# The last quarter of a fused read and expert layer: stored without a sum, in two halves

## The chip, the cores and the metric

The kernel runs on one core of a Trainium2 chip. The core has five engines with instruction streams of their own: TensorE (PE in the profile; its weight loads are shown as PEld), VectorE (DVE), ScalarE (ACT), GpSimd (POOL) and SyncE (SP), which here only issues transfers. The engines run at the same time and wait for one another through semaphores; each executes its own stream in order. Matmuls write to PSUM, which VectorE and ScalarE read; transfers go between SBUF and memory. The metric is the device time of one execution in microseconds, as the median of several.

## The reference

Two computations follow each other. First a cross read between tokens x and states, per batch and head, in both directions; then a two-layer expert layer with a parametric ReLU over all 4352 rows that come out (8 batches of 512 tokens and 32 states).

```python
scores = scale * np.matmul(x, state.transpose(0, 1, 3, 2))     # B, H = 8, 8; S, Ns, D = 512, 32, 64
a = np.exp(scores - scores.max(-1, keepdims=True))
a /= a.sum(-1, keepdims=True) + 1e-09
xread = np.matmul(a, state)
# the same with the roles of x and state exchanged gives sread
x = concatenate([xread, sread], axis=2) as rows of H * D = 512
h = x @ w_in                                                   # 512 x 2048
g = np.maximum(h, 0.0) + alpha * np.minimum(h, 0.0)
out = g @ w_out                                                # 2048 x 512
```

## The kernel before

The order of all work is written out by hand: a long string, ORDER, holds some 1100 tokens such as P.8.3.0.0, and a small interpreter at the end of the kernel calls one function for each, with the parts behind the name as arguments (line by line in the string, so this order is the order of each engine's stream). The interpreter turns a part that consists of digits into an integer and leaves any other part a string:

```python
for token in (globals().get("TOKENS") or ORDER).split():
    name, *args = token.split(".")
    steps[name](*[int(a) if a.isdigit() else a for a in args])
```

Blocks 0 to 7 are the tokens of the eight batches, 512 rows each. Block 8 is the states' rows of all batches, 256 rows, and comes last. For each block the first layer makes h in PSUM (F), ScalarE makes the negative part (N, line 630) and VectorE combines both to g (G, line 633).

The second layer, g times w_out, is done for block 0 directly (S and O) and for blocks 1 to 8 as a product of 2x2 blocks with seven products instead of eight (the quarters of the result are two row halves th by two column halves dh). The steps of a block b are:

- U.b.i.c, lines 696 to 715, on GpSimd: sums and differences of parts of g, named gsum_b_i_c. Each (i, c) has one buffer for all blocks, so U.8.4.0 overwrites what block 7's products of gsum_7_4_0 read.
- P.b.p.i.c, lines 717 to 743, on PE: product p for row tile i and half c of the inner dimension, four matmuls of 128x256. The products 1, 3, 5 and 6 go to the PSUM bank px_b, product 2 to py_b, products 4 and 7 to pv_b.
- K.b.n, line 752, on ScalarE: copies the state that px_b has reached at that point to SBUF, as kept_n_b; the following products go on adding to px_b.
- Q.b.th.dh, lines 760 to 770: forms a quarter of the result in SBUF (oq_b_th_dh) and stores it. The quarter (0, 0) is py plus kept_1, (1, 1) is pv plus kept_4, (1, 0) is pv plus kept_2, each as a sum on VectorE (line 769). The quarter (0, 1) is px itself and only copied, by the engine that the token names (line 767: v for VectorE, a for ScalarE). All stores are issued by SP, 256 KB for a block of tokens and 128 KB for block 8.

The sum Q.b.1.1 reads pv_b between two of its products: product 7 is in it, product 4 isn't yet. The products P.b.4 that follow write onto the bank that it reads. The buffers for oq are four, used in turn.

Of the kernel before, what the change touches and what calls it, by code (L numbers as in the profile page):

```python
# [30 lines left out]
F.1.7.1 N.0.13 tn.0.1.p W.3.1.p W.3.0.p tn.0.0.a N.1.7 G.0.12 G.0.13 G.1.7 F.1.3.3 N.1.3 W.2.1.p S.0.0.7 mo.1.3.a
S.0.1.6 O.0.1.v W.4.1.p F.1.5.0 N.1.5 S.0.3.6 G.1.3 G.1.5 F.1.2.1 N.1.2 G.1.2 F.1.15.4 N.1.15 F.1.12.3 G.1.15 N.1.12
G.1.12 m.1.2 F.1.6.0 N.1.6 G.1.6 F.1.14.1 N.1.14 G.1.14 mo.1.2.a S.0.0.4 S.0.0.6 O.0.0.a F.1.0.4 N.1.0 F.1.13.3 sc.2
sb.2 m.2.2.0.1 rd.1.2 mo.2.2.a.0 mo.2.2.a.1 rdo.1.a tm.2 S.0.3.7 tt.0 smax.2 S.0.3.5 O.0.3.a N.1.13 S.0.2.1.2 nb.2.a
S.0.2.5 te.2.1 S.0.2.6 S.0.2.7 te.2.0 F.1.1.0 N.1.1 G.1.13 F.1.8.1 N.1.8 G.1.0 G.1.1 F.1.4.5 S.0.2.2 m.3.2 G.1.8
N.1.4 G.1.4 F.1.10.0 lx.3 ssh.p.2 lst.1 sexp.2 mo.3.2.a ssum.2.1 tsum.2 S.0.2.4 S.0.2.0 F.1.9.5 rd.0.3 P.1.2.0.1.4
snorm.v.2 rdo.0.a N.1.9 G.1.9 S.0.2.3 N.1.10 P.1.1.0.1.3 P.1.1.1.1 P.1.2.1.1 xd.3 O.0.2.a tn.2.0.a m.2.3.1.2
mo.2.3.a.0 m.2.1 mo.2.3.a.1 wb.2 G.1.10 F.1.11.5 N.1.11 mo.2.1.a G.1.11 P.1.1.1.0 U.1.1.1.p str.1.1 sro.1.v tn.2.1.p
tt.2 F.2.15.2 F.2.1.0 P.1.2.0.0 P.1.1.0.0 F.2.14.5 m.3.1 N.2.15 N.2.1 G.2.15 K.1.1.a N.2.14 mo.3.1.a G.2.1 G.2.14
m.3.0.1.2 mo.3.0.v.1 P.1.2.1.0 F.2.11.0 U.1.3.1.p mo.3.0.a.0 U.1.2.1.p P.1.6.1.1 N.2.11 F.2.2.5 N.2.2 F.2.0.2 N.2.0  # L40
U.1.1.0.p U.1.2.0.p U.1.4.0.p lx.4 P.1.6.0.1 Q.1.0.0 G.2.11 m.5.0.1.4 mo.5.0.a.0 G.2.2 mo.5.0.a.1 rd.2.0 rdo.2.a
G.2.0 sc.3 m.3.3.5.1 mo.3.3.a.1 tm.3 mo.3.3.v.0 m.4.0.4.2 mo.4.0.a.1 sb.3 P.1.6.1.0 P.1.6.0.0 xd.4 F.2.13.0 F.2.7.1
mo.4.0.a.0 F.2.8.2 K.1.2.a P.1.5.1.0 N.2.7 nb.3.a G.2.7 N.2.13 G.2.13 N.2.8 G.2.8 F.2.9.5 N.2.9 G.2.9 te.3.0
P.1.5.0.0 smax.3 P.1.7.1.1.4 F.2.10.1 N.2.10 F.2.5.0 N.2.5 G.2.5 G.2.10 F.2.4.2 N.2.4 G.2.4 te.3.1 P.1.5.1.1
U.1.3.0.p P.1.7.1.0 P.1.5.0.1 K.1.4.a U.1.4.1.p F.2.3.5 N.2.3 G.2.3 P.1.7.0.1 F.2.6.0 N.2.6 ssh.p.3 lx.5 F.2.12.1
# [57 lines left out]
def kernel(  # L103
# [658 lines left out]
    def quarter_out(b, th, dh, e=None):  # L762
# [3 lines left out]
        if add is None:  # L766
            copier(e)(osb, pbanks[b, name])
        else:
            nc.vector.tensor_tensor(osb, pbanks[b, name], kept[b, add], ALU.add)  # L769
# [51 lines left out]
```

## Time and profile before

| what | value |
|---|---|
| median of three runs | 209.41 us (209.22 to 210.38) |
| span of the profiled execution (first to last instruction) | 207.1 us |
| median less this span | 2.3 us |
| mean granted TensorE clock | 0.996 |
| PE busy | 200.4 us, 97% |
| GpSimd, VectorE, ScalarE busy | 179.5, 171.7, 155.3 us |
| last matmul ends | 203.39 us |
| last sum on VectorE ends | 203.85 us |

The page gives no time of the profiled execution besides its span. Its parts are the busy time of each engine, the span in 40 slices, the chain of work that ended last, groups of instructions by line, and transfers. A row of the timeline gives start, duration, engine, line, operation, result and operands (buffer numbers left out) and how many instructions it holds; in brackets stands how long the engine idled ahead of it, and what ended that. The tile names there are short: px is px_7 as well as px_8, oq is any quarter.

### The profile page before, as it was taken

To read this page: it belongs to the slowest core of one execution; us is meant where nothing else is said; L and a number is where in the kernel's file an instruction comes from. 1 tells how busy PE (TensorE), PEld (TensorE's weight loads), DVE (VectorE), ACT (ScalarE), POOL (GpSimd) and SP (SyncE) were. 2 spreads that over 40 slices of the span, in tenths; PEclk is the share of its full clock that TensorE was granted. 3 is DMA by queue.
4 is the path that set the end of the run, shared out by engine and by line. 5 is a ranking of instruction groups with operands and counts; after the bars stand their busy time and mean duration, and the time that the engine had idled before them with its cause. 6 is when DMAs were issued, how large, how long until landed. Compare 5 with 4: busy or idle time off the path is not lost.

```text
span 207.1 us, 5034 instructions
## 1 busy us (share of the span) xinstructions
PE 200.4 (97%) x1997; PEld 133.6 (65%) x1997; DVE 171.7 (83%) x251; ACT 155.3 (75%) x306; POOL 179.5 (87%) x113
## 2 busy tenths in 40 slices
PE   7899999999999999999999999999999999999992
...
GB/s 175 215 207 205 204 204 97 158 173 106 178 82 101 116 192 156 53 38 167 243 118 104 148 105 0 54 103 152 55 0 53 102 0 3 0 101 104 101 77 125
DMA packets 44038, 23.68 MB, mean 114 GB/s; under 512 B 22256, under 2 KB 43504, under 8 KB 44016
## 3 DMA queue, kind: packets, MB, share of 16 engines
...
## 4 chain that ended last, share of the span: by engine, by line
PE 86%; DVE 5%; ACT 4%; DMA 2%; issue 1%; ACTq 0%
PE px L736 26%; PE h L577 24%; PE pv L736 13%; PE py L736 7%; PE m_ps L528 4%; PE h L586 3%; PE o L647 3%; DVE g L633 3%; DMA x<-in_x_dram 2%; PE sr_ps L501 2%; PE fill L253 2%; ACT neg L630 1%; PE sc L335 1%; ACT m L554 1%; PE xT_ps L320 1%
## 5 line engine op out<-in xcount | busy, mean ns | idle before, releaser
L633 DVE SCALAR_TENSOR_TENSOR g<-neg,oma_sb,h 128x512 f16<-128x512 f32 (+1 forms) x142 | 94.0, 711 | 11.6 <-ACT neg L630 11.0
L630 ACT ACTIVATE neg<-h 128x512 f32<-128x512 f32 (+1 forms) x142 | 75.6, 580 | 16.5 <-PE h L577 11.5
L577 PE MATMUL h<-aT,m 128*128 128x512 f16 x252 | 66.8, 380 | 0.1
L736 PEld LDWEIGHTS <-gsum 128*128 128x128 f16 x480 | 46.5, 98 | 13.1 <-issue 0.9
L736 PEld LDWEIGHTS <-g 128*128 128x128 f16 x360 | 34.7, 98 | 8.8 <-issue 1.4
L715 POOL TENSOR_TENSOR gsum<-g,g 128x1024 f16<-128x1024 f16 (+1 forms) x16 | 32.1, 2007 | 6.7 <-DVE g L633 4.9
L577 PEld LDWEIGHTS <-m 128*128 128x128 f16 x252 | 23.8, 98 | 18.4 <-issue 2.0
L715 POOL TENSOR_TENSOR gsum<-g,gsum 128x1024 f16<-128x1024 f16 (+1 forms) x16 | 32.0, 2005 | 1.5 <-PE px L736 1.0
L715 POOL TENSOR_TENSOR gsum<-gsum,g 128x1024 f16<-128x1024 f16 (+1 forms) x16 | 32.1, 2007 | 1.0
L736 PE MATMUL px<-ws,gsum 128*128 128x256 f16 x240 | 32.1, 273 | 0.0
L715 POOL TENSOR_TENSOR gsum<-g 128x1024 f16<-128x1024 f16 (+1 forms) x16 | 31.9, 2006 | 0.0
L752 ACT COPY kept<-px 128x512 f32<-128x512 f32 (+1 forms) x24 | 13.6, 567 | 21.0 <-PE px L736 20.9
L554 ACT CAST m<-m_ps 128x512 f16<-128x512 f32 x35 | 19.1, 602 | 1.5 <-PE m_ps L528 1.1
L769 DVE TENSOR_TENSOR oq<-pv,kept 128x512 f32<-128x512 f32 (+1 forms) x16 | 10.4, 649 | 10.6 <-PE pv L736 10.4
L736 PE MATMUL px<-w_out_sb,gsum 128*128 128x256 f16 x120 | 17.2, 273 | 0.0
L736 PE MATMUL px<-w_out_sb,g 128*128 128x256 f16 x120 | 17.2, 273 | 0.0
L405 POOL TENSOR_TENSOR ts<-ts,mx 128x1024 f32<-128x1024 f32 x7 | 13.3, 1911 | 4.4 <-DVE mx L400 4.4
L647 PE MATMUL o<-w_out_sb,g 128*128 128x512 f16 x64 | 16.6, 380 | 0.1
L736 PE MATMUL py<-w_out_sb,g 128*128 128x256 f16 x120 | 16.6, 273 | 0.0
L736 PE MATMUL pv<-ws,gsum 128*128 128x256 f16 x120 | 16.4, 273 | 0.0
L736 PE MATMUL pv<-ws,g 128*128 128x256 f16 x120 | 15.9, 273 | 0.0
L552 ACT CAST m<-m_ps 128x1024 f16<-128x1024 f32 x13 | 13.2, 1018 | 0.5 <-PE m_ps L528 0.4
...
## 6 DMA issues: line engine op xcount, KB each, us to landing
...
out_dram<-oq SPq DMA_DIRECT2D x4, 128.0 KB, 2.1
...
```

The lines of the kernel that those rows point to most:

```text
L405: engine(e).tensor_tensor(blocks(cols(live["ts", b], j, S)), blocks(scored(b, j)), over_blocks(cols(live["mx", b], j, S // N)), ALU.subtract,)
L528: nc.tensor.matmul(t[N * k : N * (k + 1), :], st_head(b, h)[64 * r : 64 * r + 64, :], w_in_sb[64 * r : 64 * r + 64, c, 512 * f : 512 * (f ...
L552: copier(e)(m_tile(b, f), t)
L554: copier(e)(m_tile(b, f)[:, g, :], t[g])
L577: nc.tensor.matmul(h.rearrange("p (r j s) -> p r j s", r=2, j=2), ms[b, f][:, g, 128 * j : 128 * (j + 1)], weights(b, g), start=(g == 0), ...
L630: nc.scalar.activation(neg, h, RELU, bias=0.0, scale=-1.0)
L633: nc.vector.scalar_tensor_tensor(g_tile(b, jc), negs.pop((b, jc)), oma_sb[:, jc : jc + 1], hs.pop((b, jc)), ALU.mult, ALU.add,)
L647: nc.tensor.matmul(outs[b, q], g_tile(b, jc)[:, 128 * q : 128 * (q + 1)], w_out_sb[:, jc, :], start=not begun and jc == 2 * jc2, stop=left ...
L715: engine(e).tensor_tensor(t, x(), y(), op)
L736: nc.tensor.matmul(pbanks[b, name][:, i, :], of(b, c)[:, j, 128 * i : 128 * (i + 1)], moving[:, 4 * c + j, :], start=not begun and j == 0, ...
L752: copier(e)(t, pbanks[b, "x"])
L769: nc.vector.tensor_tensor(osb, pbanks[b, name], kept[b, add], ALU.add)
```

## The change

Three things are written into the kernel.

First, the end of ORDER. The token P.7.3.0.0 moves behind P.8.3.0.1, and Q.7.0.1 (the copy of px_7) stays right behind it. The last product of the quarter (0, 1) of block 8, P.8.3.0.0, moves behind P.8.4.0.0, and so does its quarter's token, which is now the last of all. Second, that quarter is made in a new manner, "h": VectorE copies its left 128 columns and ScalarE its right 128, each half into its part of the same buffer, and each half is stored by a transfer of its own, the left by SP, the right by ScalarE's queue. Third, the tokens of three quarters of block 1 get a fourth part, 2, and a store of two row tiles is to be issued as two when this part is there.

```diff
-lx.4 P.1.6.0.1 Q.1.0.0 G.2.11 ...
+lx.4 P.1.6.0.1 Q.1.0.0.2 G.2.11 ...
...
-... m.6.0 Q.1.1.1 m.4.1.2.5 ...
+... m.6.0 Q.1.1.1.2 m.4.1.2.5 ...
...
-... U.2.2.1.p Q.1.1.0 U.2.4.1.p ...
+... U.2.2.1.p Q.1.1.0.2 U.2.4.1.p ...
...
-P.8.6.0.1 P.8.6.0.0 P.7.3.1.0 P.8.2.0.0 P.7.3.0.0 K.8.2.a P.8.5.0.1 U.8.3.1.p Q.8.0.0 P.8.5.0.0 K.8.4.a
-P.8.7.0.0.4 P.8.7.0.1 Q.7.0.1.v P.8.3.0.1 U.8.4.0.p Q.8.1.1 P.8.3.0.0 P.8.4.0.1 Q.8.0.1.a P.8.4.0.0 Q.8.1.0
+P.8.6.0.1 P.8.6.0.0 P.7.3.1.0 P.8.2.0.0 K.8.2.a P.8.5.0.1 U.8.3.1.p Q.8.0.0 P.8.5.0.0 K.8.4.a
+P.8.7.0.0.4 P.8.7.0.1 P.8.3.0.1 P.7.3.0.0 Q.7.0.1.v U.8.4.0.p Q.8.1.1 P.8.4.0.1 P.8.4.0.0 Q.8.1.0 P.8.3.0.0 Q.8.0.1.h
...
         osb = moe.tile([128, n_i, d_h], F32, name=f"oq_{b}_{th}_{dh}", tag="osb", bufs=4)
+        if e == "h":
+            to = quarter_rows(b, th, dh)
+            for i, (copy, queue) in enumerate(((nc.vector.tensor_copy, nc.sync), (nc.scalar.copy, nc.scalar))):
+                part = slice(d_h // 2 * i, d_h // 2 * (i + 1))
+                copy(osb[:, 0, part], pbanks[b, name][:, 0, part])
+                queue.dma_start(to[:, :, part], osb[:, 0, part])
+            return
         if add is None:
             copier(e)(osb, pbanks[b, name])
         else:
             nc.vector.tensor_tensor(osb, pbanks[b, name], kept[b, add], ALU.add)
-        nc.sync.dma_start(quarter_rows(b, th, dh), osb if b < B else osb[:, 0, :])
+        to = quarter_rows(b, th, dh)
+        if b < B and e == "2":
+            for i in range(n_i):
+                nc.sync.dma_start(to[:, i, :], osb[:, i, :])
+        else:
+            nc.sync.dma_start(to, osb if b < B else osb[:, 0, :])
```

What this makes of the streams is read from the built programs, in their order and without times. A row names the line, the operation, the result and operands and the shape, and in brackets the semaphores that it waits for. PE's last products before, one matmul of each four:

```order
L736 MATMUL py_8_3347<-w_out_sb_91,g_8_2_2977 128x256
...
L736 MATMUL px_7_3170<-w_out_sb_91,gsum_7_4_0_3305 128x256
...
L736 MATMUL px_8_3366<-ws_1_430,gsum_8_1_1_3362 128x256 [waits Activation_49]
...
L736 MATMUL px_8_3366<-ws_1_430,gsum_8_1_0_3371 128x256
...
L736 MATMUL pv_8_3442<-ws_3_604,gsum_8_3_0_3326 128x256
...
L736 MATMUL pv_8_3442<-ws_3_604,gsum_8_3_1_3431 128x256
...
L736 MATMUL px_8_3366<-w_out_sb_91,gsum_8_4_1_3392 128x256 [waits Activation_49]
...
L736 MATMUL px_8_3366<-w_out_sb_91,gsum_8_4_0_3458 128x256
...
L736 MATMUL pv_8_3442<-ws_4_570,g_8_3_2756 128x256 [waits DVE_49]
...
L736 MATMUL pv_8_3442<-ws_4_570,g_8_2_2977 128x256
```

And now (the lines stand one lower, since ORDER is one line shorter):

```order
L735 MATMUL py_8_3347<-w_out_sb_91,g_8_2_2977 128x256
...
L735 MATMUL px_8_3366<-ws_1_430,gsum_8_1_1_3362 128x256 [waits Activation_49]
...
L735 MATMUL px_8_3366<-ws_1_430,gsum_8_1_0_3371 128x256
...
L735 MATMUL pv_8_3438<-ws_3_604,gsum_8_3_0_3326 128x256
...
L735 MATMUL pv_8_3438<-ws_3_604,gsum_8_3_1_3427 128x256
...
L735 MATMUL px_8_3366<-w_out_sb_91,gsum_8_4_1_3392 128x256 [waits Activation_49]
...
L735 MATMUL px_7_3170<-w_out_sb_91,gsum_7_4_0_3305 128x256
...
L735 MATMUL pv_8_3438<-ws_4_570,g_8_3_2756 128x256 [waits DVE_49]
...
L735 MATMUL pv_8_3438<-ws_4_570,g_8_2_2977 128x256
...
L735 MATMUL px_8_3366<-w_out_sb_91,gsum_8_4_0_3458 128x256
```

The product on px_7 has moved right ahead of the pv product that waits for VectorE, and the product of gsum_8_4_0 has moved to the end.

VectorE's last rows before:

```order
L769 TENSOR_TENSOR oq_7_1_0_3402<-pv_7_3281,kept_2_7_3307 128x512 [waits DMAHW2_49,DVE_49,PE_49]
L769 TENSOR_TENSOR oq_8_0_0_3433<-py_8_3347,kept_1_8_3390 128x256 [waits DMAHW3_49,PE_49,Activation_49]
L767 COPY oq_7_0_1_3451<-px_7_3170 128x512 [waits DMAHW4_49,DVE_49,PE_49]
L769 TENSOR_TENSOR oq_8_1_1_3460<-pv_8_3442,kept_4_8_3440 128x256 [waits DVE_49,DMAHW5_49,PE_49,Activation_49]
L769 TENSOR_TENSOR oq_8_1_0_3478<-pv_8_3442,kept_2_8_3425 128x256 [waits DMAHW7_49,DVE_49,PE_49]
```

And now:

```order
L775 TENSOR_TENSOR oq_8_0_0_3429<-py_8_3347,kept_1_8_3390 128x256 [waits DMAHW3_49,PE_49,Activation_49]
L773 COPY oq_7_0_1_3455<-px_7_3170 128x512 [waits DMAHW4_49,DVE_49,PE_49]
L775 TENSOR_TENSOR oq_8_1_1_3460<-pv_8_3438,kept_4_8_3436 128x256 [waits DMAHW5_49,DVE_49,Activation_49]
L775 TENSOR_TENSOR oq_8_1_0_3471<-pv_8_3438,kept_2_8_3421 128x256 [waits DMAHW6_49,DVE_49,PE_49]
L769 COPY oq_8_0_1_3478<-px_8_3366 128x128 [waits DMAHW7_49,DVE_49,PE_49]
```

The copy of px_7 keeps its place ahead of the sum oq_8_1_1, and the copy of a half is new at the end.

ScalarE's last rows now (before, the last was one copy oq_8_0_1 of 128x256, which waited for two transfers and PE):

```order
L751 COPY kept_4_7_3352<-px_7_3170 128x512 [waits PE_49,Activation_49]
L751 COPY kept_1_8_3390<-px_8_3366 128x256 [waits DVE_49,PE_49,Activation_49]
L751 COPY kept_2_8_3421<-px_8_3366 128x256 [waits DVE_49,PE_49,Activation_49]
L751 COPY kept_4_8_3436<-px_8_3366 128x256 [waits PE_49,Activation_49]
L769 COPY oq_8_0_1_3478<-px_8_3366 128x128 [waits DMAHW5_49,DMAHW6_49,DMAHW3_49,DMAHW7_49,DMAHW1_49,DVE_49]
L770 DMA out_0_dram<-oq_8_0_1_3478 32x4x128 [waits DMAHW4_49,Activation_49]
```

The copy of the right half waits for VectorE's semaphore, and a transfer has come to ScalarE's queue. SP's last rows now:

```order
L781 DMA out_0_dram<-oq_8_0_0_3429 32x4x256 [waits DMAHW7_49,DVE_49]
L781 DMA out_0_dram<-oq_7_0_1_3455 256x1x256 [waits DMAHW0_49,DVE_49]
L781 DMA out_0_dram<-oq_8_1_1_3460 32x4x256 [waits DMAHW1_49,DVE_49]
L781 DMA out_0_dram<-oq_8_1_0_3471 32x4x256 [waits DMAHW2_49,DVE_49]
L770 DMA out_0_dram<-oq_8_0_1_3478 32x4x128 [waits DMAHW3_49,DVE_49]
```

Ahead of these, SP has the same transfers in the same shapes as before, those of block 1 among them, at one row each. The store of the half stands last on SP, behind oq_8_1_0.

More of the change, by code (lines that the diff above doesn't have):

```diff
@@ L31 @@
[L31 to L45, printed above, removed]
@@ new lines @@
+G.0.11 sc.0.1 sc.0.0 F.0.15.3 G.0.9 F.0.14.1 S.0.3.4 S.0.1.4 S.0.1.5 tm.0 tn.1.1.a tn.1.0.a tt.1 N.0.15 G.0.15 W.2.0.p
+N.0.14 G.0.14 wb.1 nb.0.a W.4.0.p F.0.13.0 te.0.1 te.0.0 tsum.0 F.0.12.3 N.0.12 S.0.0.5 S.0.1.7 m.1.3 F.1.7.1 N.0.13
+tn.0.1.p W.3.1.p W.3.0.p tn.0.0.a N.1.7 G.0.12 G.0.13 G.1.7 F.1.3.3 N.1.3 W.2.1.p S.0.0.7 mo.1.3.a S.0.1.6 O.0.1.v
+W.4.1.p F.1.5.0 N.1.5 S.0.3.6 G.1.3 G.1.5 F.1.2.1 N.1.2 G.1.2 F.1.15.4 N.1.15 F.1.12.3 G.1.15 N.1.12 G.1.12 m.1.2
+F.1.6.0 N.1.6 G.1.6 F.1.14.1 N.1.14 G.1.14 mo.1.2.a S.0.0.4 S.0.0.6 O.0.0.a F.1.0.4 N.1.0 F.1.13.3 sc.2 sb.2 m.2.2.0.1
@@ new lines @@
+P.1.1.0.0 F.2.14.5 m.3.1 N.2.15 N.2.1 G.2.15 K.1.1.a N.2.14 mo.3.1.a G.2.1 G.2.14 m.3.0.1.2 mo.3.0.v.1 P.1.2.1.0
+F.2.11.0 U.1.3.1.p mo.3.0.a.0 U.1.2.1.p P.1.6.1.1 N.2.11 F.2.2.5 N.2.2 F.2.0.2 N.2.0 U.1.1.0.p U.1.2.0.p U.1.4.0.p
+lx.4 P.1.6.0.1 Q.1.0.0.2 G.2.11 m.5.0.1.4 mo.5.0.a.0 G.2.2 mo.5.0.a.1 rd.2.0 rdo.2.a G.2.0 sc.3 m.3.3.5.1 mo.3.3.a.1
+tm.3 mo.3.3.v.0 m.4.0.4.2 mo.4.0.a.1 sb.3 P.1.6.1.0 P.1.6.0.0 xd.4 F.2.13.0 F.2.7.1 mo.4.0.a.0 F.2.8.2 K.1.2.a
+P.1.5.1.0 N.2.7 nb.3.a G.2.7 N.2.13 G.2.13 N.2.8 G.2.8 F.2.9.5 N.2.9 G.2.9 te.3.0 P.1.5.0.0 smax.3 P.1.7.1.1.4
@@ new lines @@
+F.2.10.1 N.2.10 F.2.5.0 N.2.5 G.2.5 G.2.10 F.2.4.2 N.2.4 G.2.4 te.3.1 P.1.5.1.1 U.1.3.0.p P.1.7.1.0 P.1.5.0.1 K.1.4.a
+U.1.4.1.p F.2.3.5 N.2.3 G.2.3 P.1.7.0.1 F.2.6.0 N.2.6 ssh.p.3 lx.5 F.2.12.1 N.2.12 G.2.6 P.1.7.0.0 P.1.3.1.0 m.6.0
+Q.1.1.1.2 m.4.1.2.5 sexp.3 P.1.3.1.1 mo.6.0.a G.2.12 mo.4.1.a.0 ssum.3.0 U.2.1.0.p snorm.v.3 P.1.3.0.0 P.1.4.0.0
+mo.4.1.a.1 P.1.3.0.1 U.2.2.0.p Q.1.0.1.a P.1.4.1.1 tsum.3 m.6.1.1.2 wb.3 mo.6.1.a.0 m.4.3 mo.4.3.a m.5.3.5.3 P.1.4.0.1
+mo.5.3.a.1 P.2.1.0.1.1 P.2.1.1.0 P.1.4.1.0 mo.5.3.a.0 sc.4 U.2.1.1.p U.2.2.1.p Q.1.1.0.2 U.2.4.1.p tn.3.0.p U.2.3.0.p
@@ new lines @@
+U.2.3.1.p tm.4 mo.6.1.a.1 m.4.2.0.3 mo.4.2.a.0 F.3.15.5 xd.5 N.3.15 G.3.15 F.3.1.2 F.3.8.4 N.3.1 G.3.1 N.3.8
+mo.4.2.a.1 P.2.1.0.0 F.3.12.0 N.3.12 G.3.8 nb.4.a P.2.1.1.1 F.3.7.5 G.3.12 F.3.6.3 K.2.1.a F.3.14.2 N.3.6 P.2.6.0.1
+P.2.6.1.1 sb.4 N.3.14 G.3.14 F.3.4.4 P.2.6.0.0 P.2.6.1.0 F.3.2.0 G.3.6 tn.3.1.a N.3.4 G.3.4 N.3.7 G.3.7 K.2.2.a te.4.1
+F.3.3.2 smax.4 F.3.0.3 te.4.0 N.3.3 G.3.3 N.3.2 G.3.2 P.2.5.0.0 P.2.5.0.1 P.2.5.1.0 N.3.0 P.2.5.1.1 K.2.4.a F.3.11.4
+F.3.9.5 sc.5 ssh.p.4 G.3.0 N.3.9 G.3.9 N.3.11 tt.3 G.3.11 rd.3.2 P.2.7.1.0.0 rdo.3.a F.3.10.3 N.3.10 P.2.2.1.0.5
@@ new lines @@
+P.2.2.0.0 tsum.4 P.2.2.0.1 U.2.4.0.p lx.6 P.2.7.1.1 tm.5 P.2.7.0.1 F.3.5.2 F.3.13.4 sexp.4 G.3.10 nb.5.a te.5.0
+U.3.1.0.p U.3.2.0.p N.3.5 tn.4.0.a ssum.4.3 P.2.7.0.0 P.2.3.1.1 Q.2.1.1 P.2.2.1.1 snorm.v.4 P.2.3.0.1 te.5.1 G.3.5
+P.2.3.0.0 P.2.4.0.0 P.2.4.1.1 tsum.5 tn.4.1.a P.2.3.1.0 N.3.13 tn.5.1.a tn.5.0.a tt.5 wb.4 G.3.13 P.2.4.0.1
+P.3.1.0.0.3 P.2.4.1.0 Q.2.1.0 Q.2.0.1.a P.3.1.0.1 F.4.3.2 Q.2.0.0 F.4.7.4 N.4.3 F.4.11.1 U.3.1.1.p F.4.5.0 N.4.7
+P.3.1.1.1 G.4.3 F.4.10.5 G.4.7 N.4.11 G.4.11 F.4.9.2 F.4.12.4 P.3.1.1.0 F.4.8.1 N.4.5 G.4.5 N.4.10 G.4.10 U.3.2.1.p
@@ new lines @@
+N.4.9 G.4.9 F.4.2.0 K.3.1.a U.3.4.1.p N.4.12 G.4.12 P.3.6.0.0 N.4.8 F.4.13.5 G.4.8 N.4.2 G.4.2 P.3.6.1.0 N.4.13
+P.3.6.0.1 m.7.0.2.4 mo.7.0.a.0 mo.7.0.a.1 sb.5 rd.5.1 rdo.5.a tt.4 rd.4.0 rdo.4.a xd.6 G.4.13 F.4.14.2 N.4.14
+P.3.6.1.1 F.4.15.4 K.3.2.a sc.6 G.4.14 m.6.3.1.0 tm.6 m.7.3.5.2 N.4.15 P.3.5.1.1 G.4.15 mo.7.3.a.0 mo.7.3.a.1
+U.3.3.0.p mo.6.3.a.1 P.3.5.1.0 F.4.6.5 N.4.6 F.4.4.2 N.4.4 sb.6 G.4.4 P.3.5.0.1 smax.5 lx.7 P.3.5.0.0 P.3.7.0.0.4
+K.3.4.a nb.6.a te.6.0 F.4.0.0 N.4.0 U.3.3.1.p F.4.1.2 N.4.1 mo.6.3.a.0 P.3.3.0.1 te.6.1 P.3.7.1.0 U.3.4.0.p P.3.7.1.1
@@ new lines @@
+G.5.7 U.4.2.1.p P.4.6.0.1 F.5.12.1 N.5.12 G.5.12 F.5.5.4 U.4.3.0.p F.5.9.2 N.5.5 G.5.5 N.5.9 G.5.9 P.4.6.1.1 F.5.10.5
+P.4.6.0.0 tm.7 P.4.6.1.0 F.5.8.1 N.5.10 F.5.1.4 F.5.14.2 K.4.2.a N.5.14 Q.4.0.0 G.5.14 P.4.5.1.1 U.4.3.1.p P.4.5.1.0
+P.4.5.0.0 G.5.10 nb.7.a wb.6 te.7.0 P.4.5.0.1 N.5.1 te.7.1 tsum.7 F.5.4.3 G.5.1 N.5.8 G.5.8 P.4.7.0.0.2 F.5.11.5
+N.5.11 G.5.11 K.4.4.a tn.7.0.a P.4.7.0.1 P.4.7.1.1 P.4.7.1.0 F.5.6.4 N.5.6 U.4.4.1.p P.4.3.0.1 P.4.3.1.1 tn.6.1.p
+F.6.2.1 N.6.2 U.4.4.0.p P.4.3.0.0 P.5.1.1.0.5 P.4.3.1.0 sb.7 Q.4.1.1 P.4.4.1.1 P.4.4.0.1 G.6.2 G.5.6 smax.7 P.4.4.0.0
@@ new lines @@
+P.4.4.1.0 tn.6.0.a Q.4.0.1.a Q.4.1.0 N.5.4 G.5.4 F.6.4.1 N.6.4 G.6.4 P.5.1.0.0 F.6.9.0 F.6.1.4 N.6.9 G.6.9 F.5.13.2
+N.5.13 tt.6 tn.7.1.p G.5.13 F.6.5.3 N.6.5 G.6.5 U.5.1.0.p P.5.1.1.1 F.6.14.1 P.5.1.0.1 U.5.2.0.p ssh.p.7 F.6.3.0
+F.6.12.2 N.6.14 G.6.14 P.5.2.0.1.3 P.5.2.1.1 tt.7 F.6.6.1 K.5.1.a P.5.6.0.0 P.5.6.1.0 P.5.2.1.0 N.6.3 G.6.3 N.6.1
+N.6.12 G.6.1 N.6.6 G.6.6 G.6.12 U.5.1.1.p U.5.2.1.p sexp.7 P.5.2.0.0 m.7.1.0.4 mo.7.1.a.1 mo.7.1.a.0 Q.5.0.0 rd.7.1
+rdo.7.a rd.6.2 rdo.6.a ssum.7.3 snorm.v.7 P.5.6.0.1 P.5.6.1.1 K.5.2.a F.8.2.4 F.8.12.0 N.8.2 G.8.2 F.6.8.1 N.6.8 G.6.8
@@ new lines @@
+F.6.15.2 N.8.12 G.8.12 U.5.4.1.p F.6.7.3 N.6.7 G.6.7 F.8.6.4 P.5.5.0.1 wb.7 F.6.13.1 N.6.13 U.5.3.1.p P.5.7.0.1.0
+P.5.7.1.1 N.8.6 G.8.6 G.6.13 P.5.5.1.0 U.5.3.0.p P.5.5.1.1 F.8.1.3 N.8.1 P.5.7.0.0 P.5.7.1.0 F.8.3.4 N.6.15 G.6.15
+N.8.3 U.5.4.0.p P.5.5.0.0 F.6.0.1 K.5.4.a G.8.3 F.8.0.2 U.6.1.1.p G.8.1 P.5.3.0.0 Q.5.1.1 N.6.0 F.7.3.4 U.6.2.1.p
+N.8.0 G.8.0 F.8.4.3 P.5.3.0.1 F.6.10.2 G.6.0 P.5.3.1.1 N.6.10 G.6.10 N.7.3 N.8.4 G.8.4 P.5.4.0.0 U.6.4.1.p F.6.11.1
+N.6.11 P.5.3.1.0 Q.5.0.1.a F.7.14.2 P.5.4.0.1 G.6.11 G.7.3 P.5.4.1.0 P.5.4.1.1 Q.5.1.0 U.6.1.0.p N.7.14 G.7.14
@@ new lines @@
+F.7.13.3 N.7.13 F.7.8.5 G.7.13 F.7.7.1 N.7.7 G.7.7 F.8.11.4 N.7.8 F.7.12.0 G.7.8 N.8.11 F.7.4.2 N.7.4 G.7.4 U.6.2.0.p
+G.8.11 P.6.1.1.0.3 U.6.3.1.p U.6.4.0.p F.8.15.1 P.6.1.0.1 F.8.8.5 N.8.8 N.8.15 P.6.1.0.0 P.6.1.1.1 K.6.1.a F.8.14.2
+F.7.5.4 N.7.12 N.7.5 P.6.6.0.0 G.7.12 G.8.8 P.6.6.1.0 G.7.5 P.6.6.0.1 F.7.6.0 N.7.6 P.6.7.1.1.5 P.6.7.0.1 G.8.15
+U.6.3.0.p G.7.6 U.7.3.1.p P.6.6.1.1 K.6.2.a F.7.0.4 N.7.0 F.8.10.1 G.7.0 N.8.10 G.8.10 P.6.5.1.0 N.8.14 G.8.14
+F.7.15.0 N.7.15 G.7.15 P.6.5.0.1 F.7.2.4 F.7.11.1 F.8.13.2 N.7.2 G.7.2 P.6.5.1.1 U.7.1.1.p N.8.13 G.8.13 N.7.11 G.7.11
@@ new lines @@
+P.6.7.1.0 F.7.1.0 N.7.1 F.8.5.4 N.8.5 G.7.1 F.7.10.2 U.7.2.1.p N.7.10 G.7.10 P.6.5.0.0 K.6.4.a P.6.2.0.0.1 G.8.5
+F.7.9.0 P.6.2.1.1 P.7.1.0.1.2 P.7.1.0.0 N.7.9 P.6.2.0.1 G.7.9 P.6.2.1.0 P.6.7.0.0 F.8.9.4 P.6.3.0.1 P.7.2.0.0.0
+P.6.3.0.0 U.7.1.0.p Q.6.1.1 P.7.1.1.1 P.6.4.0.0 P.6.4.0.1 P.6.4.1.0 Q.6.0.0 P.6.4.1.1 Q.6.1.0 P.7.1.1.0 U.7.3.0.p
+P.6.3.1.0 F.8.7.1 P.6.3.1.1 P.7.2.1.0 U.7.2.0.p K.7.1.a P.7.6.1.1 P.7.6.0.0 N.8.7 G.8.7 P.7.7.0.0.5 P.7.6.0.1
+P.7.6.1.0 P.7.7.1.0 P.7.2.0.1 Q.6.0.1.v U.7.4.0.p K.7.2.a P.7.5.1.1 P.7.5.0.1 U.7.4.1.p N.8.9 G.8.9 P.7.5.1.0
```

73 lines of the change are left out of this document (16 added, 57 removed).

## The prediction

> **What bounds the kernel now.** I read the page's head and slices first, then the chain of waits over the last 7 us, because the diff touches little else.
>
> ```profile
> span 207.1 us, 5034 instructions
> PE 200.4 (97%) x1997; PEld 133.6 (65%) x1997; DVE 171.7 (83%) x251; ACT 155.3 (75%) x306; POOL 179.5 (87%) x113
> ...
> PE   7899999999999999999999999999999999999992
> ```
>
> ```profile
> 199.90 0.87 PE px L736 x8
> 200.77 0.87 PE pv L736 x8
> 201.64 0.87 PE px L736 x8
> 202.52 0.89 PE pv L736 x8
> 203.40 0.02 issue
> 203.43 0.42 DVE oq L769
> ```
>
> TensorE (PE) is busy 97% of the span, and in every slice but the first and last. The end is a chain: PE's last products, one VectorE sum of 0.42 us, then a store. So whatever delays PE near the end is paid in full, and whatever shortens the work behind its last product is gained in full. The timeline there, in start, duration, engine:
>
> ```profile
> 199.29 0.60 PE L736 MATMUL px<-w_out_sb,gsum 128*128 128x256 f16 x4
> 199.73 1.04 PE L736 MATMUL px<-ws,gsum 128*128 128x256 f16 x8
> 200.60 1.04 PE L736 MATMUL pv<-ws,gsum 128*128 128x256 f16 x8
> 201.48 1.04 PE L736 MATMUL px<-w_out_sb,gsum 128*128 128x256 f16 x8
> 202.35 1.04 PE L736 MATMUL pv<-ws,g 128*128 128x256 f16 x8
> ...
> 199.55 0.42 DVE L769 TENSOR_TENSOR oq<-py,kept 128x256 f32<-128x256 f32 x1 [1.11 <-PE py L736]
> 199.93 0.69 DVE L767 COPY oq<-px 128x512 f32<-128x512 f32 x1
> 201.74 0.42 DVE L769 TENSOR_TENSOR oq<-pv,kept 128x256 f32<-128x256 f32 x1 [1.11 <-PE pv L736]
> 203.43 0.42 DVE L769 TENSOR_TENSOR oq<-pv,kept 128x256 f32<-128x256 f32 x1 [1.26 <-PE pv L736]
> ...
> 200.04 1.15 POOL L715 TENSOR_TENSOR gsum<-g,gsum 128x512 f16<-128x512 f16 x1 [1.04 <-PE px L736]
> ```
>
> A product of four matmuls takes PE 0.437 us (eight stand 0.87 apart), and the last of its matmuls ends 0.60 us after the first begins. PE's last end is 202.35 + 1.04 = 203.39. In this order the row at 199.29 is P.7.3.0.0, the last product of px_7. Three things hang on it or follow it: VectorE's copy of px_7 (Q.7.0.1) at 199.93; GpSimd's gsum_8_4_0 (U.8.4.0), which overwrites the one buffer that this product reads and starts 0.15 us after it; and on VectorE, in program order behind the copy, the sum Q.8.1.1 at 201.74. PE's pv products P.8.4.0.1 and P.8.4.0.0 (the row at 202.35) write onto the bank that this sum reads, so they must come after it. They do, by 202.35 - 202.16 = 0.19 us, and PE waits for nothing.
>
> **The change, part by part.**
>
> *The early stores.* The three tokens end in "2". The interpreter turns digits into integers, and the new code asks e == "2", a string. So the branch is never taken; SyncE's (SP's) rows up to the last few are the same in both programs. Cost 0, with nothing to hide.
>
> *P.7.3.0.0 goes five products later*, behind P.8.5.0.1, P.8.5.0.0, P.8.7.0.0, P.8.7.0.1 and P.8.3.0.1. Those five start 0.437 earlier each, with the same lead over what releases them; no new wait there. It itself starts at 199.29 + 5 x 0.437 = 201.48 and ends at 202.08. VectorE takes up a finished product 0.04 after its end (203.39 to 203.43), so the copy of px_7 runs from 202.12 to 202.81. The sum Q.8.1.1 is queued behind it and could before start at 201.74; now it runs from 202.81 to 203.23. PE's P.8.4.0.1 is next in PE's order, due at 201.48 + 0.437 = 201.92, and must wait for that sum. The handover from VectorE to PE, seen early in the kernel:
>
> ```profile
> 5.38 0.96 DVE L189 CAST xg<-x 128x512 f16<-128x512 f32 x2 [5.38 <-DMA x<-in_x_dram]
> ...
> 6.39 0.23 PEld L320 LDWEIGHTS <-xg 128*128 128x128 f16 x4 [0.30 <-DVE xg L189]
> ```
>
> The casts end at 6.34 and the weights behind them load at 6.39: 0.05 us. So P.8.4.0.1 starts at 203.28, a stall of 1.36 us where there was none. Could it be less? Back-to-back VectorE rows above start 0.38 apart for a 0.42 us instruction, which would give 1.32; a slower handover of 0.1 would give 1.41. I take 1.36.
>
> U.8.4.0 is moved with it: it waits for P.7.3.0.0, runs from 202.08 + 0.15 = 202.23 to 203.38, and P.8.3.0.0, now PE's last product, needs its result. That product would come at 203.28 + 2 x 0.437 = 204.15, so the sum of GpSimd is hidden by the stall. Were the stall gone, it would be what is late next: P.8.3.0.0 due at 202.79 would start at 203.38 + 0.05 = 203.43, 0.64 us late. PE's last end becomes 204.15 + 0.60 = 204.75, that is +1.36.
>
> The 256 KB store of px_7 is issued 2.19 us later, with two 128 KB stores behind it on SP. SP issues one in some 0.55 us (row below): 202.83, 203.38, and the third when its sum ends (204.35 + 0.42 = 204.77). SP is free again at 205.32. No engine waits for these.
>
> *The last quarter.* Removed from the path: the sum of 0.42 us, which now runs at 204.35 beside PE's last product. Added: a VectorE copy of 128x128, a ScalarE copy of 128x128, and a store by each engine's queue, 64 KB each. ScalarE's copy stands in the built program behind a wait for VectorE's semaphore, and the only VectorE instruction left to wait for is the other half's copy. So I take the halves one after the other.
>
> ```profile
> L767 DVE COPY oq<-px 128x512 f32<-128x512 f32 x2 | 1.4, 688 | 0.0
> L474 DVE RECIPROCAL r<-r 128x2 f32<-128x2 f32 x8 | 1.2, 145 | 0.0
> L769 DVE TENSOR_TENSOR oq<-py,kept 128x256 f32<-128x256 f32 x1 | 0.4, 425 | 1.1 <-PE py L736 1.1
> ...
> L454 ACT ACTIVATE nb<-nb 128x2 f32<-128x2 f32 x8 | 1.7, 208 | 0.0
> L767 ACT COPY oq<-px 128x256 f32<-128x256 f32 x1 | 0.4, 372 | 1.3 <-PE px L736 1.3
> L275 ACT CAST st<-st 128x128 f16<-128x128 f32 x1 | 0.3, 292 | 0.0
> ```
>
> No 128x128 copy runs on VectorE: between 0.145 (two columns) and 0.425 (256). The line through 256 and 512 columns gives 0.29, which I take. ScalarE: between 0.208 and 0.372; the cast of the same size took 0.292, taken as 0.28. So 204.75 + 0.04 + 0.29 = 205.08 for the first half, + 0.05 + 0.28 = 205.41 for the second; before, the last data stood ready at 203.43 + 0.42 = 203.85. That is +1.56; by the bounds of the two copies +1.34 to +1.79, and +1.23 if the halves ran side by side. The Trainium skill, PSUM — Partial Sum Buffer, section "PSUM bank collisions raise a hardware error", says that two engines must not access one bank in the same 32 partitions at once, two reads included, and that a semaphore has to keep them apart. By that rule the split saves nothing over one copy; the sum with halves side by side would be 0.33 us less. The trace of before has no pair of such reads.
>
> ```profile
> L770 SPq DMA_DIRECT2D out_dram<-oq x8: 534/546/574, 193.2 to 203.9; - x8
> DMA to landing us min/median/max: 2.1/2.3/2.5
> ...
> L183 ACTq DMA_DIRECT2D x<-in_x_dram x2: 558/563/568, 1.3 to 1.9; - x2
> L196 ACTq DMA_DIRECT2D st<-in_state_dram x1: 487/487/487, 0.7 to 0.7; - x1
> ```
>
> ```profile
> GB/s 0 0 0 212 344 344 334 61 0 0 0 288 314 46 217 344 339 339 56 0 0 40 339 263 5 106 359 182 0 5 303 309 31 0 0 0 0 0 0 0
> out_dram<-oq SPq DMA_DIRECT2D x4, 128.0 KB, 2.1
> ```
>
> Issues cost the same on ScalarE's queue as on SP's (0.49 to 0.57). A 128 KB store lands 2.1 us after issue. In the bandwidth row (40 slices of 0.2 us from 199 us on) its data moves only in the last full pair of slices, some 0.5 us. Half the bytes save 0 to 0.26. SP issues its half at 205.32, ScalarE at 205.43, so both halves move at the same time and together are 128 KB again: I take 2.0, bounds 1.84 and 2.3. The last landing goes from 203.87 + 2.1 = 205.97 to 207.43: +1.46. What follows the landing, 207.1 - 205.97 = 1.1 us of closing, I leave as it is.
>
> *Sum*, against the profiled execution's own 207.1 us: +1.36 (stall) - 0.42 + 0.29 + 0.05 + 0.28 (copies for the sum) - 0.1 (half stores) = +1.46, a span of 208.6 us. The median of the runs, 209.41, lies 2.3 above the span; I take that as unchanged: 209.41 + 1.46 = 210.9 us, +0.7%. The likeliest case's own bounds: the low ends of copies, stall and store (-0.22, -0.04, -0.16) give 210.5, the high ends (+0.23, +0.05, +0.3) 211.5.
>
> **The rivals.**
>
> *Not slower: PE does not wait.* The one mechanism: the wait before P.8.4.0.1 is satisfied by an earlier VectorE instruction, or VectorE reaches Q.8.1.1 in time. It decides at 201.92 - 0.42 - 0.05 = 201.45: if that sum starts by then, PE goes on. Then P.8.3.0.0 waits at most for U.8.4.0. Without that either, the end moves by -0.42 + 0.29 + 0.05 + 0.28 - 0.1 = +0.1, 209.5 us; with it, +0.1 + 0.64, 210.1. For it: before, the same wait cost nothing. Against: the copy queued ahead on VectorE cannot begin before 202.08. Chance 0.10.
>
> *The clock falls in the stall.* The granted clock by stretch:
>
> ```profile
> 204.00:205.00 1.00, 0.00 (x0) 0.00 (x0) 0.00 (x0) 0.00 (x0) 0.00 (x0) 1.00 0.38 131
> 205.00:206.00 1.00, 0.00 (x0) 0.00 (x0) 0.00 (x0) 0.00 (x0) 0.00 (x0) 0.76 0.38 131
> 206.00:207.10 1.10, 0.00 (x0) 0.00 (x0) 0.00 (x0) 0.00 (x0) 0.00 (x0) 0.50 0.00 0
> ```
>
> PE ends at 203.39; the clock is whole until 205, then 0.76 in the mean of a stretch and 0.50, so it falls near 205.5, after 2.1 us of rest. A stall of 1.36 is shorter. If it fell all the same, the twelve matmuls behind it would take 2 x 1.31 us: 212.2. Chance 0.04. The Trainium skill, TensorE: Matmul & The Clock Gate, section "HAM oscillation", asks for no gap over some 3.4 us; by that too the clock stays.
>
> *ScalarE's copy waits for the first half's store.* Its row names DMAHW3, the semaphore that SP's half store raises. That store's own row waits for the same one, so I read it as an earlier round. If not, the copy starts after a landing near 207.4 and the end moves 2 us on: 212.9. Chance 0.03.
>
> *The early stores are split after all.* These are three of SP's first four stores of oq.
>
> ```profile
> 58.36 0.65 SPq L770 DMA_DIRECT2D out_dram<-oq  x1
> 71.12 5.84 SPq L770 DMA_DIRECT2D out_dram<-oq  x3
> ...
> SPq L770 <- DVE oq L769: 73.7, 21, 18.1
> ```
>
> That would be three more issues of 0.55 us between 58 and 77 us, on a queue that waits 73.7 us in all for such sums. So it adds nothing to the forecast, and the time is 210.9 too. Chance 0.03.
>
> **How the numbers follow.** The forecast has 0.80, the rivals 0.10, 0.04, 0.03 and 0.03. Of this kernel 0.5%, 1.05 us, can about be told from no change, so slower begins at 210.46. The likeliest case's own range is 210.5 to 211.5, down to 210.1 with the halves side by side (-0.33), and some 0.1 of its 0.80 lies under 210.46, since its runs spread by 1.2 us. Slower: 0.70 + 0.04 + 0.03 + 0.03 = 0.80. Same: 0.10 of the forecast and most of the first rival, 0.18. Faster than 208.4 no case gives; 0.02 is left for it. For 8 in 10 the range leaves out the dear rivals (0.07) and the cheap half of the first (0.05): 210.1 to 211.6.
>
> **What would show it.** Right: in the tail a px row between the px and pv rows of PE, then a gap of 1.3 to 1.4 us on PE, put down to VectorE's oq; the copy of px_7 near 202.1; ScalarE's half starting as VectorE's ends; two 64 KB stores, one of them ScalarE's; 28 stores of 256 KB as before. Wrong: PE without a gap, halves that overlap, six 128 KB stores in the middle of the kernel, or a difference that lies ahead of 198 us, where both programs run the same instructions in the same order.

## The result and the profile after

The changed kernel takes 210.81 us in the median (210.68 to 210.94, six runs) against 209.28 for the kernel before in the same set of runs (209.07 to 210.38): 1.5 us more, a ratio of 1.0072 with a 95% interval of 1.0055 to 1.0089. The forecast was 210.9.

The page of the changed kernel, its head and the slices of PE:

```profile
span 209.0 us, 5039 instructions
PE 201.2 (96%) x1997; PEld 134.1 (64%) x1997; DVE 172.1 (82%) x252; ACT 155.1 (74%) x306; POOL 179.6 (86%) x113
...
PE   7999999999999999999999999999999999999972
```

The slice before the last, full before, is down to seven tenths: TensorE (PE) rests near the end. The chain of waits there, start, duration, what:

```profile
201.47 0.89 PE px L735 x8
202.36 0.02 issue
202.38 0.06 DVE oq L773
...
202.99 0.43 DVE oq L775
203.42 0.04 issue
203.46 1.05 PE pv L735 x8
204.51 0.02 issue
204.53 0.44 DVE oq L775
204.97 0.00 issue
204.97 0.30 DVE oq L769
205.27 0.02 issue
205.29 0.27 ACT oq L769
```

Before, the chain ran on PE up to 203.40 and through one sum. Now it leaves PE at 202.36 for VectorE's copy of px_7 (L773) and the sum behind it (L775), comes back to PE at 203.46, and ends with two copies one after the other. The rows of the timeline, with what ended the idle time in brackets:

```profile
199.56 1.04 PE L735 MATMUL px<-ws,gsum 128*128 128x256 f16 x8
200.44 1.04 PE L735 MATMUL pv<-ws,gsum 128*128 128x256 f16 x8
...
201.31 1.04 PE L735 MATMUL px<-w_out_sb,gsum 128*128 128x256 f16 x8
...
202.38 0.69 DVE L773 COPY oq<-px 128x512 f32<-128x512 f32 x1 [2.14 <-PE px L735]
202.49 1.16 POOL L714 TENSOR_TENSOR gsum<-g,gsum 128x512 f16<-128x512 f16 x1 [3.19 <-PE px L735]
202.99 0.41 DVE L775 TENSOR_TENSOR oq<-pv,kept 128x256 f32<-128x256 f32 x1
203.46 1.03 PE L735 MATMUL pv<-ws,g 128*128 128x256 f16 x8 [1.11 <-DVE oq L775]
...
204.33 0.60 PE L735 MATMUL px<-w_out_sb,gsum 128*128 128x256 f16 x4
...
204.97 0.29 DVE L769 COPY oq<-px 128x128 f32<-128x128 f32 x1
205.29 0.27 ACT L769 COPY oq<-px 128x128 f32<-128x128 f32 x1 [4.23 <-DVE oq L769]
205.59 0.66 ACTq L770 DMA_DIRECT2D out_dram<-oq  x1
205.64 0.56 SPq L770 DMA_DIRECT2D out_dram<-oq  x1
```

The eight matmuls at 201.31 are P.8.3.0.1 and P.7.3.0.0; their successor was due 0.875 later, at 202.19, and started at 203.46. That is a stall of 1.27 us. The bracket says 1.11 since it counts from the modelled end of the last matmul.

The two profiled executions are not level ahead of this place. The row at 199.29 before (the product behind py_8) stands at 199.56 here. So 0.27 us of the 1.9 between the spans of 207.1 and 209.0 came earlier, where PE's work is the same in both programs. The prediction names a difference ahead of 198 us as a sign of being wrong, but this one is a scatter of the start: the first product of block 1 into py stands at 48.99 and 49.26, and from there to the row above both take 150.30 us. That execution of the kernel before was a quick one (three later sets of eighteen runs each have a median span near 207.4). From here on, differences are counted from that row.

The two stores by queue, size and time to landing:

```profile
out_dram<-oq ACTq DMA_DIRECT2D x1, 64.0 KB, 2.3
out_dram<-oq SPq DMA_DIRECT2D x1, 64.0 KB, 1.9
```

ScalarE's store, issued at 205.59, lands last, near 207.9; the closing is again 1.1 us.

### The profile page after: what moved, and what is told of

Its sections match the earlier page's. It is cut to its first block, busy times and chain, and to the rows that moved or that the text cites. A ratio compares the mean times of both kernels' runs of the same rounds, so it can differ in the third digit from the quotient of the medians.

```text
span 209.0 us, 5039 instructions
## 1 busy us (share of the span) xinstructions
PE 201.2 (96%) x1997; PEld 134.1 (64%) x1997; DVE 172.1 (82%) x252; ACT 155.1 (74%) x306; POOL 179.6 (86%) x113
## 4 chain that ended last, share of the span: by engine, by line
PE 80%; ACT 6%; DMA 5%; DVE 5%; issue 1%; POOL 1%; POOLq 0%; DVEq 0%; SPq 0%
PE px L735 24%; PE h L576 23%; PE pv L735 13%; PE py L735 6%; PE m_ps L527 4%; PE h L585 3%; DMA w_in_sb<-in_moe_w_in_dram 3%; PE o L646 3%; DVE g L632 3%; DMA xT<-xg 2%; PE sr_ps L500 1%; ACT neg L629 1%; ACT m L553 1%; ACT m L551 1%; PE sc L334 1%
## 5 line engine op out<-in xcount | busy, mean ns | idle before, releaser
L775 DVE TENSOR_TENSOR oq<-pv,kept 128x512 f32<-128x512 f32 (+1 forms) x16 | 10.4, 649 | 9.3 <-PE pv L735 9.2
```

## The experiments

Theory S: the late product P.7.3.0.0 makes PE wait, by VectorE's queue. Rival H: the halves and the second queue are the loss. Rival G: the halves gain, and only the move loses. In the diffs stand the tokens of ORDER in which a run differs.

**The move undone.** From the changed kernel:

```diff
-P.8.2.0.0 K.8.2.a ... P.8.7.0.1 P.8.3.0.1 P.7.3.0.0 Q.7.0.1.v U.8.4.0.p
+P.8.2.0.0 P.7.3.0.0 K.8.2.a ... P.8.7.0.1 Q.7.0.1.v P.8.3.0.1 U.8.4.0.p
```

> The changed kernel with the product P.7.3.0.0 and the copy of px_7 put back where they stood before; the last quarter stays last, in halves. Theory S (the stall of PE behind the late copy of px_7 is the loss): no gap on PE in the tail, so 1.27 us are gone. What is left against before is the end behind the last product: halves 0.29 + 0.03 + 0.27 for a sum of 0.42 (+0.17) and a landing of 2.3 for 2.1 (+0.2): 209.3 + 0.4 = 209.7 us. Rival H (the halves and the second queue are the loss): stays at 210.5 or above. Rival G (halves gain, as they are meant to, and only the move loses): below 209.3.

Measured: 209.74 us, ratio to before 1.0032 (1.0016 to 1.0048), so 0.59 above before and 1.07 under the changed kernel. Most of the loss is the move's. The timeline shows that one part of the expectation was wrong:

```profile
201.78 0.60 PE L735 MATMUL px<-w_out_sb,gsum 128*128 128x256 f16 x4
202.03 0.42 DVE L775 TENSOR_TENSOR oq<-pv,kept 128x256 f32<-128x256 f32 x1 [1.11 <-PE pv L735]
202.51 1.03 PE L735 MATMUL pv<-ws,g 128*128 128x256 f16 x8
203.38 0.60 PE L735 MATMUL px<-w_out_sb,gsum 128*128 128x256 f16 x4
```

There is a gap after all: P.8.4.0.1 was due at 201.78 + 0.44 = 202.22 and starts at 202.51, when the sum Q.8.1.1 has ended at 202.45. Before, two products stood between P.8.7.0.1, which releases that sum, and P.8.4.0.1, which needs it done; with P.8.3.0.0 moved to the end only one is left. That is 0.29 us for the second move by itself, in this order. The rest, 0.31, is the end: the span ends 4.02 us after PE's last matmul (203.98 to 208.0), 3.71 before (203.39 to 207.1).

**The move alone.** From the kernel of before:

```diff
-P.8.2.0.0 P.7.3.0.0 K.8.2.a ... P.8.7.0.1 Q.7.0.1.v P.8.3.0.1 U.8.4.0.p
+P.8.2.0.0 K.8.2.a ... P.8.7.0.1 P.8.3.0.1 P.7.3.0.0 Q.7.0.1.v U.8.4.0.p
```

> The kernel of before with P.7.3.0.0 and the copy of px_7 moved behind P.8.3.0.1 and nothing else. Theory S: the product of gsum_8_4_0 stands next on PE and waits for GpSimd, which can begin only after P.7.3.0.0: 202.08 + 0.15 + 1.15 + 0.07 = 203.45 instead of 201.92, so PE stalls 1.5 us, the sum on VectorE is done meanwhile, and the end is that of before: 209.3 + 1.5 = 210.8 us. Rival H: no change, 209.3.

Measured: 210.68 us, ratio 1.0071 (1.005 to 1.0092). Without any halves, a loss of the same size is there, but by the other wait, behind GpSimd:

```profile
202.53 1.15 POOL L714 TENSOR_TENSOR gsum<-g,gsum 128x512 f16<-128x512 f16 x1 [3.21 <-PE px L735]
...
203.74 0.61 PE L735 MATMUL px<-w_out_sb,gsum 128*128 128x256 f16 x4 [1.36 <-POOL gsum L714]
```

GpSimd's sum waits for P.7.3.0.0 to have read the buffer, and P.8.3.0.0 waits for the sum: due at 201.35 + 0.875 = 202.22, it starts 1.52 us late. The end behind PE (205.23 to 208.9, 3.67) is that of before.

**One copy for the halves.** From the changed kernel:

```diff
-P.8.3.0.0 Q.8.0.1.h
+P.8.3.0.0 Q.8.0.1.a
```

> The changed kernel with the last quarter copied whole by ScalarE and stored in one transfer by SyncE; the order stays. Theory S: the gap of 1.27 us on PE stays. The end behind the last product is 0.03 + 0.37 for 0.04 + 0.29 + 0.03 + 0.27 (-0.23) and a landing of 2.1 for 2.3 (-0.2): 210.8 - 0.4 = 210.4 us. Rival H: back to 209.3 to 209.7. Rival G: the halves save something, so this is above 210.8.

Measured: 210.98 us, ratio 1.0092 (1.0067 to 1.0116): not below the changed kernel, as I had expected, but 0.17 above it in the medians. The gap on PE is the same. In the end behind it (206.22 to 210.1 in the profiled execution, 3.88 us against 4.07) 0.19 is saved and not 0.4. The rows of SyncE's transfer queue (SP) show a part of why, first its last two issues together, then the last alone:

```profile
206.27 1.21 SPq L781 DMA_DIRECT2D out_dram<-oq  x2
...
206.93 0.55 SPq L781 DMA_DIRECT2D out_dram<-oq  x1
```

The copy ends at 206.25 + 0.37 = 206.62, but SP is still issuing the store of Q.8.1.0 and takes up the last one at 206.93, 0.31 after the copy's end. The second queue of the changed kernel avoids just that. The rest of the miss lies outside of what the trace shows: the time exceeds the span by 2.06 to 2.14 us in all six runs, by 1.75 to 1.84 in those of the changed kernel. I can't say why.

**The late copy given to ScalarE.** From the changed kernel:

```diff
-Q.7.0.1.v U.8.4.0.p Q.8.1.1
+Q.7.0.1.a U.8.4.0.p Q.8.1.1
```

> The changed kernel with only the late copy of px_7 given to ScalarE instead of VectorE. Theory S, as worked out: VectorE has nothing ahead of the sum Q.8.1.1, which runs near 201.4, so PE does not wait at P.8.4.0.1; what is late next is P.8.3.0.0, which waits for GpSimd's sum until 203.45 instead of 202.79. The gap on PE goes from 1.27 to 0.65 and moves one place back: 210.8 - 0.6 = 210.2 us. Rival: the wait at P.8.4.0.1 is for the late product itself or for something else than the queue on VectorE: the gap and 210.8 us stay.

Measured: 210.11 us, ratio 1.0049 (1.0031 to 1.0066).

```profile
201.59 0.42 DVE L775 TENSOR_TENSOR oq<-pv,kept 128x256 f32<-128x256 f32 x1 [1.32 <-PE pv L735]
202.21 1.04 PE L735 MATMUL pv<-ws,g 128*128 128x256 f16 x8
...
202.52 1.16 POOL L714 TENSOR_TENSOR gsum<-g,gsum 128x512 f16<-128x512 f16 x1 [3.21 <-PE px L735]
...
203.73 0.61 PE L735 MATMUL px<-w_out_sb,gsum 128*128 128x256 f16 x4 [0.49 <-POOL gsum L714]
```

The sum runs early, the pv products start on time, and the gap moves to P.8.3.0.0: due at 203.08, started at 203.73, 0.65 us, where the prediction had named 0.64 as late next.

**Two VectorE instructions exchanged.** From the changed kernel:

```diff
-Q.7.0.1.v U.8.4.0.p Q.8.1.1
+U.8.4.0.p Q.8.1.1 Q.7.0.1.v
```

> The changed kernel with two VectorE instructions exchanged: the sum Q.8.1.1 ahead of the late copy of px_7. Nothing is removed and no engine changes. If place on VectorE's queue is what makes PE wait at P.8.4.0.1, this is e4 again: PE goes on there, the gap left is that ahead of P.8.3.0.0, 0.65 us, behind GpSimd's sum: 210.1 us. If e4 gained because VectorE had less work or for another reason, the gap of 1.27 and 210.8 us stay.

Measured: 210.03 us, ratio 1.0052 (1.0034 to 1.0071), the same as with ScalarE. The sum runs early again, ahead of the copy, and the pv products start on time:

```profile
201.53 0.42 DVE L775 TENSOR_TENSOR oq<-pv,kept 128x256 f32<-128x256 f32 x1 [1.32 <-PE pv L735]
202.15 1.04 PE L735 MATMUL pv<-ws,g 128*128 128x256 f16 x8
202.35 0.69 DVE L773 COPY oq<-px 128x512 f32<-128x512 f32 x1 [0.39 <-PE px L735]
```

The only wait of PE from 196 us on is for GpSimd:

```profile
PE px L735 <- POOL gsum L714: 0.5, 1, 0.5
```

VectorE does the same work as in the changed kernel, the copy of 0.69 us included. So it is the place on VectorE's queue, not its load, that made PE stand still.

**The early stores really split.** From the changed kernel:

```diff
-        if b < B and e == "2":
+        if b < B and e == 2:
```

> The changed kernel with the comparison made against the integer 2, so that the three stores of block 1 really go out in two pieces each. Theory: SyncE waits for most of the kernel, three more issues of 0.55 us between 58 and 77 us cost nothing: 210.8 us as the changed kernel, within 0.3. Rival: a transpose of x stands right behind two of these stores on SyncE and comes 0.55 us later, PE waits for it, and the time is above 211.3; or smaller stores free their buffers earlier and the time is below 210.4.

Measured: 210.48 us, ratio 1.0064 (1.0051 to 1.0077), 0.33 under the changed kernel's 210.81: just outside the 0.3 of the forecast, and not under the 210.4 of the rival. So the split was put into the kernel of before as well, and the changed kernel was run again beside it on one chip, another than that of e5.

```diff
-Q.1.0.0 ... Q.1.1.1 ... Q.1.1.0
+Q.1.0.0.2 ... Q.1.1.1.2 ... Q.1.1.0.2     # with the comparison against the integer
```

> The kernel of before with the three stores of block 1 really issued in two pieces each, and nothing else. Run e5, with the split and the tail of the change, came out at 210.48 against 210.81 for the tail alone, on another day's runs. If the split gains 0.3 us (its pieces free the four buffers of oq earlier, or its transfers collide less), this is 208.9 against 209.2 and beats both kernels. If it costs nothing and gains nothing, as forecast, it is 209.2 and the 0.3 is scatter between sets of runs.

> The changed kernel as it is, once more, beside e10 on one chip: 210.8 us by the first measurement. If sets of runs differ by 0.3 us it may come out at 210.5, and then e5 says nothing on the split.

Measured: 208.95 against 209.12 us, ratio 0.9996 (0.9986 to 1.0006), and 210.73 for the changed kernel, near the first 210.81. By the ratio, the split in the kernel of before isn't told from no change; by the medians, the kernels with it are 0.17 and 0.25 us below those without. The traces show where this doesn't come from. From the first product of block 1 into py to the one into py_8, PE takes 149.86 us with the split (e5, 49.08 to 198.94; e10, 49.21 to 199.07) and 149.87 without (before, 48.99 to 198.86; after, 49.26 to 199.13). So the smaller stores make nothing start earlier in between. What is shorter in these single executions is the end behind PE's last matmul: 3.76 us in e5 (204.74 to 208.5) against 4.07 after, 3.50 in e10 (203.60 to 207.1) against 3.71 before. Why, and whether it always is, isn't shown. In the changed kernel as it stands the split doesn't happen.

**One copy in the undone order.** Run e1 with the last token Q.8.0.1.a for Q.8.0.1.h.

> Run e1_move_undone with the last quarter copied whole by ScalarE and stored in one transfer by SyncE. In e1 PE still stood still for 0.29 us ahead of P.8.4.0.1, since P.8.3.0.0 no longer covers the sum Q.8.1.1; that gap stays here. Against before: gap +0.29, copy 0.03 + 0.37 for a sum of 0.04 + 0.42 (-0.06), and the last store is issued only when SyncE is through with the store of Q.8.1.0, issued 0.43 us after that product's end for 0.55 us: some 0.18 late. 209.15 + 0.41 = 209.6 us, like e1. If instead the halves with their two queues are dearer than one copy, it is below 209.4; if cheaper, above 209.9.

Measured: 210.02 us, ratio 1.0038 (1.0025 to 1.0051), 0.28 above e1 in the medians, so the forecast of 209.6 was missed towards dearer. Its median span is 207.9, against 208.0 for e1; as in e3, the time exceeds the span by 2.07 to 2.13 us instead of 1.73 to 1.84. By the span, one copy and two halves cost the same; what makes the one copy dearer lies outside the span and is not explained.

**An order without gaps.** From the changed kernel, with the last store on ScalarE's queue:

```diff
-P.8.2.0.0 K.8.2.a P.8.5.0.1 U.8.3.1.p Q.8.0.0 P.8.5.0.0 K.8.4.a P.8.7.0.0.4 P.8.7.0.1 P.8.3.0.1 P.7.3.0.0 Q.7.0.1.v
-U.8.4.0.p Q.8.1.1 P.8.4.0.1 P.8.4.0.0 Q.8.1.0 P.8.3.0.0 Q.8.0.1.h
+P.7.3.0.0 K.8.2.a P.8.5.0.1 U.8.3.1.p P.8.5.0.0 K.8.4.a P.8.7.0.0.4 P.8.7.0.1 P.8.3.0.1 U.8.4.0.p Q.7.0.1.v Q.8.1.1
+P.8.2.0.0 P.8.4.0.1 Q.8.0.0 P.8.4.0.0 Q.8.1.0 P.8.3.0.0 Q.8.0.1.q     # q: copy and store by ScalarE
```

> A new order for the tail, with the last quarter last, copied whole by ScalarE and stored in one transfer by ScalarE's queue: P.7.3.0.0 early (so GpSimd's sum is done in time), and P.8.2.0.0 moved between P.8.3.0.1 and P.8.4.0.1, so that two products cover the sum Q.8.1.1. By the theory PE has no gap at all and ends as before; behind it stand 0.03 + 0.37 for 0.04 + 0.42 us, and the store waits for no other issue: 209.15 - 0.06 = 209.1 us, the same as before. With a landing on ScalarE's queue of 2.3 for 2.1: 209.3. A gap that is left would show at 209.5 or above.

Measured: 209.45 us, ratio 1.0027 (1.0004 to 1.0049). PE's rows follow one another 0.44 us per product to the end:

```profile
201.29 0.60 PE L735 MATMUL px<-w_out_sb,gsum 128*128 128x256 f16 x4
...
201.73 0.60 PE L735 MATMUL py<-w_out_sb,g 128*128 128x256 f16 x4
202.17 1.04 PE L735 MATMUL pv<-ws,g 128*128 128x256 f16 x8
...
203.04 0.60 PE L735 MATMUL px<-w_out_sb,gsum 128*128 128x256 f16 x4
```

With the sum Q.8.1.1 covered by two products and GpSimd's sum released early, the last quarter can stand last with no gap. The median span, 207.5, is about that of before (207.4), and the end behind PE's last matmul, 3.76 us (203.64 to 207.4), that of before too: the copy is 0.05 shorter than the sum, the landing 0.1 longer. The median time is 0.27 above before, and its interval just leaves out no change. So dropping the last sum gains nothing, even where it costs nothing on PE. No run is told faster than the kernel of before; the lowest median, e10's, is 0.17 under it, with an interval on both sides of no change.

## Why the prediction was right

*The stall.* Forecast 1.36, measured 1.27. The chain was the forecast one: product late, copy late, sum queued behind it, PE waiting. The difference is VectorE's two instructions, which started 0.61 apart (202.38 to 202.99), where I had added the copy's full 0.69. The two exchanges (e4, e7) show that the queue is the cause. Run e2 shows that the move alone loses as much, but not by this queue: there GpSimd's sum is the wait, and that 1.52 us of it come out near the 1.27 here and 0.36 at the end is chance.

*GpSimd's sum as late next.* It was hidden in the changed kernel, ending at 202.49 + 1.16 = 203.65 with P.8.3.0.0 at 204.33, and came out with the forecast 0.64 (0.65) once the stall was gone.

*The copies.* Forecast 0.29 and 0.28, one after the other; measured 0.29 and 0.27, with ScalarE released by VectorE's half. The rule of the Trainium skill, PSUM — Partial Sum Buffer, section "PSUM bank collisions raise a hardware error", agrees with this order. In all five traces with halves (after, e1, e4, e5, e7) ScalarE's half starts 0.03 to 0.04 us behind the end of VectorE's. That the shared bank is the reason isn't shown, since no run has the halves in two banks; halves side by side were not tried.

*The stores.* This term was mis-sized. I took 2.0 us for the half stores, inside bounds of 1.84 to 2.3. SP's half took 1.9, ScalarE's, which ends the kernel, 2.3. So the second transfer lost 0.2 against one store of 2.1 instead of saving 0.1. From PE's last matmul to the end of the span it is 4.07 us, where 3.71 stood before and 3.81 was forecast. This loss is not a constant: in the other runs with halves ScalarE's half landed after 2.3 (e1), 2.2 (e4, e5) and 2.0 us (e7), and the end took 4.02, 3.96, 3.76 and 3.83.

*The sum.* 1.27 + (4.07 - 3.71) = 1.63 us by the traces against 1.46 forecast; 1.53 by the medians. The stall came out smaller and the stores dearer, and the errors partly cancel; that the forecast of 210.9 is met within 0.1 is in part luck. The 2.3 us that were kept between span and median set the span of a quick execution against a median. Run by run, the time exceeds the span by 1.72 to 1.85 us in the later runs of the kernel before and by 1.75 to 1.84 in those of the changed kernel, so leaving the term unchanged was right, though its size wasn't.

*The early stores.* As read from the code, they were not split: 28 stores of 256 KB of oq before and after.

*The rivals.* The clock did not fall in the stall: the stretch from 204 to 205 us has 1.00 granted, in the midst of the matmuls behind it.

```profile
204.00:205.00 1.00, 0.93 (x9) 0.59 (x6) 0.46 (x2) 0.00 (x0) 0.00 (x0) 1.00 0.67 232
...
207.00:208.00 1.00, 0.00 (x0) 0.00 (x0) 0.00 (x0) 0.00 (x0) 0.00 (x0) 0.87 0.33 97
```

ScalarE's copy did not wait for the first half's store, which was issued after that copy had ended. The rival in which PE does not wait at P.8.4.0.1 was priced at 210.1 with GpSimd's sum late; e4 and e7, which take the copy out of the sum's way, make that case and took 210.11 and 210.03. What I overlooked is that P.8.3.0.0, when it goes last, no longer covers the sum Q.8.1.1. In the changed order P.7.3.0.0 has come into its place and covers it, so e4 and e7 have no gap at P.8.4.0.1, and the forecast was not touched. Only where P.7.3.0.0 goes back, in e1 and e6, do the 0.29 us show, and there my expectation for e1 of no gap was wrong.
